# Merging two 256-column steps of a layer into one of 512 columns

## The chip, the cores and the metric

The kernel runs on one core of a Trainium2 chip. The metric is the device time of one execution in microseconds; each version is run several times and the median is compared. Besides, one execution of each version is recorded by the hardware profiler, and the rows shown below come from that.

## The reference

Three stages follow each other, all in fp32. Attention has 4 batches of 8 heads with 576 positions of width 64; of each row of scores only the 32 largest are kept before the softmax. Its output is laid out as 2304 tokens of width 512. Two feed-forward layers follow: layer 1 has 512 to 2048 to 512 with a piecewise function between, layer 2 is gated, with 512 to 1536 to 512.

```
scores = scale * q @ k^T;  kth = 32nd largest of each row
attn = softmax(where(scores >= kth, scores, -1e9));  a = attn @ v
x = a.transpose(0, 2, 1, 3).reshape(2304, 512)
h = x @ w_in
g = where(h >= 1, h, where(h <= -1, 0, (h + 1)**2 / 4));  x2 = g @ w_out
out = (silu(x2 @ w_gate) * (x2 @ w_val)) @ w_out2
```

## The kernel before, in words

**Numbers.** Each fp32 operand of a layer's matmul is split into a high and a low half of TensorE's fp32r type (tile `w`, 128 x 2 x 512), and a product takes three matmuls: high by high, low by high, high by low (`PASSES`). `hilo` (L797 on ACT for the high half, L799 on POOL for the low one) makes the split of activations, `convert` (L762 to L774) that of weights. A converted weight tile is kept in DRAM (`ws_...`) and loaded again, 512 KB, by every later step that needs it (`weight`).

**Attention.** It runs in 32 units: batch, block of query tiles, pair of heads. The blocks of batches 0 to 2 are query tiles (0, 1) and then (2, 3, 4), 256 and 320 columns; those of batch 3 the other way round. A unit has four or five score tiles, 144 in all. For each, PE makes 128 x 576 scores in a pair of PSUM banks `pS` (L612; there are two such pairs), DVE finds the 32nd largest with four MAX8 (L626) and three MATCH_REPLACE8 (L636) and masks with it (L640), ACT takes the exponential (L633). PE then transposes (L687 to L707), multiplies by the values (L567, L569), and the result goes to DRAM as `xs` (store `xs<-y`), by units.

**Layers.** The 2304 tokens are cut into sub-blocks of columns, seven of 256 and a last one, number 7, of 512 (`SUBS`). The list `STEPS` gives the layer steps in program order: layer 1 and 2 of 0, of 1, of 2, then layer 1 of 3, layer 1 of 4, layer 2 of (3, 4), layer 1 of 5, layer 1 of 6, layer 2 of (5, 6), layer 1 of 7, layer 2 of 7. A step's input of layer 1 is loaded from `xs` (`t<-xs`) and needs all four units (pairs of heads) of the attention blocks that its columns touch.

A PSUM bank `pM` holds 512 columns. Where a step has 256 columns, `lanes` puts two units of the wide dimension side by side in one bank (F = 2); where it has two sub-blocks of 256, the two stand side by side (F = 1). In either case `proj` (matmuls at L877) goes through the lanes one by one, four slices k of 128 and three passes each, so that every matmul of such a step has 256 columns. Only sub-block 7 has matmuls of 512 columns there. Behind `proj` of layer 1 come relu, square and gmax (L936, L938, L940) and the split; four finished groups of 128 make a slab, for which `x2_part` multiplies by the second matrix (L913) in the same lanes. Its sums go through `accumulate` (L807 to L815) into `big`, of which there are two; after the last slab `hilo` splits the sum into one wide buffer for each bank of 512 columns, and `self.x2` notes where each slice of each sub-block lies. For a single sub-block of 256 columns a buffer thus holds two slices of it side by side.

Layer 2 projects with gate and value weights (also L877), combines (L996, L998, L1008), splits, and `out_part` (L974) multiplies 128 rows at a time by 512 columns. The rings that matter: 15 wide buffers `w` for weights, inputs and split activations, two banks `pM`, two `big`.

**Order.** Nothing of the order is written by hand. `Plan` collects all operations with modelled durations; `forward` is a list schedule by priority with rings that are handed out in order of creation; `backward` schedules the reversed graph, and its begins are the priorities of the next forward round. `schedule` makes one forward plan from fixed priorities and up to four rounds from backward ones, and keeps the shortest by the model. Each engine then executes its instructions in that fixed order, and all transfers are issued in order on SP's queue.

Of the kernel before, what the change touches and what calls it, by code (L numbers as in the profile page):

```python
# [54 lines left out]
class Op:  # L55
    __slots__ = ("eng", "dur", "fn", "deps", "prio", "seq", "opens", "bufs", "left", "users", "ready", "start", "end", "lat", "tag")


class Plan:
# [9 lines left out]
    def __init__(self):  # L69
        self.ops = []  # L70
        self.rings = []

    def ring(self, *a, **k):
        r = Ring(*a, **k)
        self.rings.append(r)
        return r

    def op(self, eng, dur, fn, reads=(), writes=(), prio=5, tag="", lat=None):
        o = Op()
        o.eng, o.dur, o.fn, o.prio, o.seq, o.tag = eng, dur, fn, self.PRI.get(tag, prio), len(self.ops), tag  # L80
        o.lat = self.LAT if lat is None else lat
        deps = set()
# [119 lines left out]
    def backward(self):  # L202
# [37 lines left out]
        while True:  # L240
# [30 lines left out]
            while events and events[0][0] <= now + 1e-9:  # L271
# [10 lines left out]
                for d in ops[s].deps:  # L282
                    heapq.heappush(events, (now + (0.0 if ops[d].eng == ops[s].eng == "PE" else ops[d].lat), 1, d))

    def schedule(self):

        best, least = self.forward(), self.length
        for _ in range(self.ROUNDS):
            begin = self.backward()
            if begin is None:  # L290
                break
            for o in self.ops:
                o.prio = -begin[o.seq]
# [11 lines left out]
class Kernel:  # L305
    SUBS = (256, 256, 256, 256, 256, 256, 256, 512)
    STEPS = ((1, (0,)), (2, (0,)), (1, (1,)), (2, (1,)), (1, (2,)), (2, (2,)), (1, (3,)), (1, (4,)), (2, (3, 4)),
             (1, (5,)), (1, (6,)), (2, (5, 6)), (1, (7,)), (2, (7,)))

    BLOCKS = (((0, 1), (2, 3, 4)), ((0, 1), (2, 3, 4)), ((0, 1), (2, 3, 4)), ((2, 3, 4), (0, 1)))  # L310
    KV = 4
    AV_POOL = True

    SAME, SWAP = (slice(0, 128), slice(0, 128), 0), ((slice(0, 64), slice(64, 128), 1), (slice(64, 128), slice(0, 64), 1))
# [19 lines left out]

    SB, FN, PS = 0.043, 0.136, 0.065

# [18 lines left out]
    def build(self):  # L355
# [29 lines left out]
        self.p_m = R("pM", [128, 512], F32, 4 - self.PT_BANKS, "P")  # L385
        self.xdeps = {}
        self.attention()
# [3 lines left out]
    def attention(self):  # L391
# [4 lines left out]
        def ready(u):  # L396
            b, hp, blk = units[u]
            if blk == 0:
                state["kv", b, hp] = self.prep(b, hp)
            state["q", u] = self.prep_q(b, hp, self.BLOCKS[b][blk])  # L400

        ready(0)
# [37 lines left out]

    def prep(self, b, hp):

        nc, p, T = self.nc, self.p, self.t
        kT = self.r_kT.new()
        V = self.r_v.new()

        raw = self.load_raw(T["k"], b, hp)
# [21 lines left out]
        raw = self.load_raw(T["v"], b, hp)  # L469
        self.split(raw, V)  # L470
        return kT, V

# [81 lines left out]
    def outputs(self, b, hp, blk, V, PT, rs, rc):  # L554
# [29 lines left out]
        p.op("POOL", self.pool(N), lambda: nc.gpsimd.tensor_tensor(  # L584
            out=y[:, 0:N], in0=y[:, 0:N], in1=rb[:, 0:N], op=OP.mult), [rb], [(y, None)], 2, "norm")
        key = (hp, b, blk)
        xs = self.t["xs"][key]
# [139 lines left out]

    def convert(self, ring, kind, f, early=False):

# [28 lines left out]
        def flat():  # L758
            return W[:].rearrange("p s n -> p (s n)").bitcast(F32) if ring is not None else W[:]


        p.op("ACT", self.act(512, self.SB), lambda: nc.scalar.activation(  # L762
            out=word(0), in_=cv[:].bitcast(U16).rearrange("p (n t) -> p n t", t=4)[:, :, 1], func=AF.Copy,
            scale=2.0 ** -13, bias=2.0 ** -14 - 0.5), [], [(cv, 0)], 3, tag + "cvl")
        p.op("ACT", self.act(512, self.SB), lambda: nc.scalar.activation(
            out=ct[:], in_=word(1, F32), func=AF.Sign), [(cv, 1)], [ct], 3, tag + "cvs")
        p.op("DVE", self.dve(512), lambda: nc.vector.scalar_tensor_tensor(  # L767
            out=word(0), in0=word(1), scalar=3, in1=word(0),
            op0=OP.logical_shift_left, op1=OP.bitwise_or), [(cv, 1)], [(cv, 0)], 3, tag + "cvt")
        p.op("POOL", self.pool(512), lambda: nc.gpsimd.tensor_tensor(  # L770
# [23 lines left out]

    def hilo(self, src, dst, n, prio=3, off=0, key=None):
        nc, p = self.nc, self.p
        p.op("ACT", self.act(n, self.SB), lambda: nc.scalar.activation(out=dst[:, 0, 0:n], in_=src[:, off:off + n], func=AF.Copy),  # L797
             [(src, key)], [(dst, 0)], prio, "hi")
        p.op("POOL", self.pool(n), lambda: nc.gpsimd.tensor_tensor(  # L799
            out=dst[:, 1, 0:n], in0=src[:, off:off + n], in1=dst[:, 0, 0:n].bitcast(F32), op=OP.subtract),  # L800
            [(src, key), (dst, 0)], [(dst, 1)], prio, "lo")

# [31 lines left out]
    def moe(self):  # L834
# [5 lines left out]
        for f in range(self.HELD[0]):  # L840
            self.held["moe_w_in", f] = self.convert(self.r_w, "moe_w_in", f)
            if f < self.HELD[1]:
                self.held["moe_w_out", f] = self.convert(self.r_w, "moe_w_out", f)
# [3 lines left out]
        for u in units[:e1] + units[n1:n1 + e2]:  # L847
            self.convert(None, *u, early=True)
        self.later = units[n1 + e2:][:self.PRE]
# [24 lines left out]

# [7 lines left out]
    def layer1(self, subs):  # L882
        nc, p, T = self.nc, self.p, self.t
        F, lanes, w = self.lanes(subs)
        X = {}
        for kk in range(KC // F):
            xf = self.r_t.new()
            x = self.r_w.new()
# [12 lines left out]
        def x2_part(slab):  # L901
            for f in range(4 * slab, 4 * slab + 4):
                WO[f] = self.weight(self.r_w, "moe_w_out", f)
            for jj in range(KC // F):
                ps = self.p_m.new()
                for u, i, at, n in lanes:
                    for q in range(4):
                        f = 4 * slab + q
                        bank, gat = self.place(subs, f)[i]

                        def mms(f=f, q=q, j=jj * F + u, at=at, n=n, ps=ps, g=G[bank], gat=gat):
# [3 lines left out]
                        p.op("PE", self.mm(n, 3), mms, [WO[f], G[bank]] + [(ps, 0)] * (at > 0), [(ps, at)], 5, "x2")  # L915
                if jj % 2 == 0 and slab == 0:
# [196 lines left out]
```

## Time and profile before

| what | value |
|---|---|
| median of three runs | 1344.08 us (1342.28 to 1344.23) |
| the profiled execution's own time | 1339.11 us |
| its span, first to last instruction | 1337.3 us |
| PE, DVE, ACT, POOL busy | 91%, 77%, 65%, 59% |
| mean granted TensorE clock | 0.962 |
| DMA | 329 MB, 246 GB/s on the mean |

Times are microseconds. PE is TensorE's matmul, PEld its weight load, DVE is VectorE, ACT is ScalarE, POOL is GpSimd, SP is the engine whose queue issues the transfers. L877 is line 877 of the kernel before. The duration of one matmul in a row reaches from its start to its modelled end and overlaps the next one; a matmul's pitch is read where many follow back to back.

### The profile page before, as it was taken

To read this page: it belongs to the slowest core of one execution; us is meant where nothing else is said; L and a number is where in the kernel's file an instruction comes from. 1 tells how busy PE (TensorE), PEld (TensorE's weight loads), DVE (VectorE), ACT (ScalarE), POOL (GpSimd) and SP (SyncE) were. 2 spreads that over 40 slices of the span, in tenths; PEclk is the share of its full clock that TensorE was granted. 3 is DMA by queue.
4 is the path that set the end of the run, shared out by engine and by line. 5 is a ranking of instruction groups with operands and counts; after the bars stand their busy time and mean duration, and the time that the engine had idled before them with its cause. 6 is when DMAs were issued, how large, how long until landed. Compare 5 with 4: busy or idle time off the path is not lost.

```text
span 1337.3 us, 24475 instructions
## 1 busy us (share of the span) xinstructions
PE 1220.9 (91%) x8408; PEld 1126.8 (84%) x8408; DVE 1032.1 (77%) x2066; ACT 875.2 (65%) x1916; POOL 785.7 (59%) x821
## 2 busy tenths in 40 slices
PE   2566588998899999999999999999999999999998
PEld 1445388887799999998999999999999999877887
DVE  5989999999999999999999988999999212122222
ACT  6888799888877678776778777668775321342211
POOL 8977669799956466765577755646554313223111
PEclk9965689999999999999999999999999999999999
DMA  8878778989868796878686844367668554655454
GB/s 294 271 263 282 238 269 279 350 291 326 290 229 308 243 346 216 341 258 304 224 306 244 309 138 167 94 207 278 231 260 312 196 195 184 210 206 198 146 189 157
DMA packets 138188, 329.29 MB, mean 246 GB/s; under 512 B 21200, under 2 KB 67792, under 8 KB 138064
## 3 DMA queue, kind: packets, MB, share of 16 engines
q1 hardware_dynamic: 138064, 327.73, 69.3%
q8 instruction: 66, 1.08, 0.3%
q14 instruction: 58, 0.48, 0.1%
HBM read 282.59 MB, written 45.09 MB: 245 GB/s over the span
## 4 chain that ended last, share of the span: by engine, by line
PE 67%; DVE 9%; ACT 8%; DMA 8%; POOL 4%; issue 3%; SPq 0%; DVEq 0%; ACTq 0%; POOLq 0%
PE pM L877 31%; PE pM L913 12%; PE pM L974 10%; PE pS L612 4%; PE pT L567 4%; DVE v L626 3%; DVE R L636 3%; PE pT L687 3%; DVE cv L767 2%; DMA w<-ws_moe_w_in 1%; DMA cv<-in_moe_w_in_dram 1%; DMA w<-ws_moe_w_out 1%; ACT qT L489 1%; POOL ct L770 1%; ACT cv L762 1%
## 5 line engine op out<-in xcount | busy, mean ns | idle before, releaser
L877 PE MATMUL pM<-w,w 128*128 128x256 f32 (+1 forms) x3840 | 564.4, 300 | 3.2 <-POOL w L799 1.8
L877 PEld LDWEIGHTS pM<-w,w 128*128 128x128 f32 x3840 | 512.1, 192 | 25.2 <-POOL w L799 2.7
L799 POOL TENSOR_TENSOR w<-t,w 128x512 fp32r<-128x512 f32 x144 | 186.9, 1301 | 267.4 <-ACT w L797 240.5
L626 DVE MAX8 v<-R 128x8 f32<-128x576 f32 x432 | 314.8, 748 | 1.1
L913 PE MATMUL pM<-w,w 128*128 128x256 f32 (+1 forms) x1536 | 228.6, 300 | 4.0 <-DVE t L940 2.0
L676 POOL TENSOR_TENSOR PT<-F,PT 128x384 fp32r<-128x384 f32 (+2 forms) x192 | 176.3, 927 | 72.5 <-ACT F L674 66.6
L913 PEld LDWEIGHTS pM<-w,w 128*128 128x128 f32 x1536 | 203.4, 190 | 16.1 <-DVE t L940 4.9
L636 DVE MATCH_REPLACE8 R<-v,R 128x576 f32<-128x576 f32 x288 | 213.3, 741 | 0.0
L974 PE MATMUL pM<-w,w 128*128 128x512 f32 x648 | 160.9, 396 | 2.0 <-DVE t L998 0.9
L797 ACT ACTIVATE w<-t 128x512 fp32r<-128x512 f32 x144 | 91.1, 637 | 94.9 <-DVE t L1008 74.6
L974 PEld LDWEIGHTS pM<-w,w 128*128 128x128 f32 x648 | 118.1, 188 | 25.8 <-POOL w L774 1.6
L626 DVE MAX8 v<-pS 128x8 f32<-128x576 f32 x144 | 109.1, 758 | 32.8 <-PE pS L612 30.2
L612 PE MATMUL pS<-kT,qT 128*128 128x288 f32 x512 | 104.7, 328 | 18.4 <-DVE E L640 16.0
L633 ACT ACTIVATE E<-pS,nb 128x576 f32<-128x576 f32 x144 | 107.3, 745 | 21.1 <-DVE R L636 12.2
L687 PE MATMUL pT<-idf,E 128*128 128x128 f32 x512 | 97.5, 298 | 24.7 <-ACT qz L501 7.8
L640 DVE SCALAR_TENSOR_TENSOR E<-pS,v,E 128x576 f32<-128x576 f32 x144 | 115.7, 803 | 0.4
L998 DVE SCALAR_TENSOR_TENSOR t<-t,pM 128x512 f32<-128x512 f32 x54 | 36.8, 681 | 95.9 <-ACT t L996 95.7
L672 ACT ACTIVATE PT<-pT 128x384 fp32r<-128x384 f32 (+2 forms) x192 | 87.8, 460 | 32.5 <-PE pT L687 18.1
L636 DVE MATCH_REPLACE8 R<-v,pS 128x576 f32<-128x576 f32 x144 | 107.5, 746 | 0.0
L770 POOL TENSOR_TENSOR ct<-ct,cv 128x512 int32<-128x512 int32 x68 | 92.0, 1357 | 22.5 <-DVE cv L767 9.9
L612 PEld LDWEIGHTS pS<-kT,qT 128*128 128x128 f32 x512 | 83.2, 210 | 24.8 <-DVE E L640 20.7
L687 PEld LDWEIGHTS pT<-idf,E 128*128 128x128 f32 x512 | 66.2, 151 | 35.0 <-ACT qT L489 9.3
(83 smaller groups left out, 1772.3 us busy)
## 6 DMA issues: line engine op xcount, KB each, us to landing
w<-ws_moe_w_out SPq DMA_DIRECT2D x184, 512.0 KB, 6.1
w<-ws_moe_w_in SPq DMA_DIRECT2D x118, 512.0 KB, 5.5
w<-ws_moe_w_gate SPq DMA_DIRECT2D x67, 512.0 KB, 5.7
w<-ws_moe_w_val SPq DMA_DIRECT2D x66, 512.0 KB, 6.3
cv<-in_moe_w_out_dram SPq DMA_DIRECT2D x28, 512.0 KB, 4.9
cv<-in_moe_w_in_dram SPq DMA_DIRECT2D x16, 512.0 KB, 5.1
ws_moe_w_out<-w SPq DMA_DIRECT2D x16, 512.0 KB, 5.0
ws_moe_w_out<-cv SPq DMA_DIRECT2D x12, 512.0 KB, 3.4
```

Of the source, the lines that this page charges most:

```text
L612: nc.tensor.matmul(ps[:, j, 0:288], l(), kT[:, hh, at + j * 288:at + (j + 1) * 288], start=k == 0, stop=k == len(lhs) - 1)
L626: p.op("DVE", self.dve(576) + (0 if k else self.PS), lambda: nc.vector.max(out=v8[:, h, k, :], in_=rr() if k else sc()), [Rb if k else ps] ...
L633: p.op("ACT", self.act(576, self.FN - self.SB), lambda h=h, sc=sc, ee=ee: nc.scalar.activation(out=ee(), in_=sc(), func=AF.Exp, bias=nb[:, ...
L636: p.op("DVE", self.dve(576) + 0.06 + (0 if k else self.PS), lambda h=h, k=k, sc=sc, rr=rr: nc.vector.match_replace(out=rr(), in_to_replace ...
L640: p.op("DVE", self.dve(576) + 0.06 + self.PS, lambda h=h, sc=sc, ee=ee: nc.vector.scalar_tensor_tensor(out=ee(), in0=sc(), scalar=v8[:, h, ...
L676: p.op("POOL", self.pool(n), lambda: nc.gpsimd.tensor_tensor(out=dst(1), in0=src(F), in1=dst(0).bitcast(F32), op=OP.subtract), [F, (PT, (0 ...
L687: fn = (lambda ps=ps, m=m, h=h, c=c: nc.tensor.transpose(ps[:, m * 128:(m + 1) * 128], Sb[:, h, 64 * h + c * 128:64 * h + (c + 1) * 128], ...
L770: p.op("POOL", self.pool(512), lambda: nc.gpsimd.tensor_tensor(out=ci(), in0=ci(), in1=word(0), op=OP.add), [(cv, 0)], [ct], 3, tag + "cvadd")
L799: p.op("POOL", self.pool(n), lambda: nc.gpsimd.tensor_tensor(out=dst[:, 1, 0:n], in0=src[:, off:off + n], in1=dst[:, 0, 0:n].bitcast(F32), ...
L877: nc.tensor.matmul(ps[:, at:at + n], W[:, w, k * 128:(k + 1) * 128], x[:, s, xat:xat + n], start=k == 0 and j == 0, stop=k == KC - 1 and j ...
L913: nc.tensor.matmul(ps[:, at:at + n], WO[f][:, v, j * 128:(j + 1) * 128], g[:, s, gat:gat + n], start=q == 0 and m == 0, stop=q == 3 and m ...
L974: nc.tensor.matmul(ps[:], a[:, s, at:at + 128], WO[f][:, v, :], start=q == 0 and m == 0, stop=q == 3 and m == 2)
```

## The change

Sub-blocks 5 and 6 are one step of layer 1. Where two neighbouring lanes belong to the same unit and their inputs adjoin in the same buffer, the new function `joined` makes them one lane, and `proj` and `x2_part` then issue one matmul of 512 columns for two of 256. So that the input of layer 2 of (3, 4) adjoins too, layer 1 of 3 splits each slice of its result into the left half of a buffer of its own, and layer 1 of 4 fills the right half. `hilo` has a column offset for the destination.

```diff
-             (1, (5,)), (1, (6,)), (2, (5, 6)), (1, (7,)), (2, (7,)))
+             (1, (5, 6)), (2, (5, 6)), (1, (7,)), (2, (7,)))
+    JOIN = True
...
-    def hilo(self, src, dst, n, prio=3, off=0, key=None):
+    def hilo(self, src, dst, n, prio=3, off=0, key=None, to=0):
         nc, p = self.nc, self.p
-        p.op("ACT", self.act(n, self.SB), lambda: nc.scalar.activation(out=dst[:, 0, 0:n], in_=src[:, off:off + n], func=AF.Copy),
-             [(src, key)], [(dst, 0)], prio, "hi")
+        p.op("ACT", self.act(n, self.SB), lambda: nc.scalar.activation(out=dst[:, 0, to:to + n], in_=src[:, off:off + n], func=AF.Copy),
+             [(src, key)], [(dst, (0, to))], prio, "hi")
...
+    @staticmethod
+    def joined(lanes, where):
+
+        out = []
+        for u, i, at, n in lanes:
+            x, xat = where(u, i)
+            if out and out[-1][0] == u and out[-1][3] is x and out[-1][1] + out[-1][2] == at and out[-1][4] + out[-1][2] == xat:
+                out[-1][2] += n
+            else:
+                out.append([u, at, n, x, xat])
+        return out
...
-        for u, i, at, n in lanes:
+        both = [self.joined(lanes, lambda u, i, k=k: X[k, i]) for k in range(KC)]
+        for m in range(len(both[0])):
             for k in range(KC):
-                x, xat = X[k, i]
+                u, at, n, x, xat = both[k][m]
...
                 if slab == FF1 // 512 - 1:
-                    x = self.r_w.new()
-                    self.hilo(acc[jj // 2], x, w, off=off, key=jj % 2)
+                    pair = [s for layer, s in self.STEPS if layer == 2 and subs[0] in s][0]
+                    if pair == subs or not self.JOIN:
+                        x = self.r_w.new()
+                        self.hilo(acc[jj // 2], x, w, off=off, key=jj % 2)
+                        for u, i, at, n in lanes:
+                            self.x2[jj * F + u, i] = (x, at)
+                        continue
+
                     for u, i, at, n in lanes:
-                        self.x2[jj * F + u, i] = (x, at)
+                        j, to = jj * F + u, sum(self.SUBS[s] for s in pair if s < i)
+                        if to == 0:
+                            self.x2[j, i] = (self.r_w.new(), 0)
+                        x = self.x2[j, pair[0]][0]
+                        self.x2[j, i] = (x, to)
+                        self.hilo(acc[jj // 2], x, n, off=off + at, key=jj % 2, to=to)
```

The loop over lanes of `x2_part` is changed as that of `proj`. `schedule` keeps the first plan made from backward priorities even if the plan from fixed priorities was shorter, and from there on the shortest:

```diff
         best, least = self.forward(), self.length
+        first = None
         for _ in range(self.ROUNDS):
...
-            if self.length < least:
-                best, least = order, self.length
+            if self.length < least or first is None:
+                best, least, first = order, self.length, [o.prio for o in self.ops]
```

The rest of the diff adds switches that are off (`rush`, `FIRST`, `QFIRST`, `DIRECT`, `VIA`, `BANKED`, `AHEAD`, `PORT` = 0) and splits `prep` into its key and value parts, called one after the other as before.

## Rows read from the trace of the kernel before

**Rows 1.** The page's first lines: span, and busy time of each engine.

```profile
span 1337.3 us, 24475 instructions
...
PE 1220.9 (91%) x8408; PEld 1126.8 (84%) x8408; DVE 1032.1 (77%) x2066; ACT 875.2 (65%) x1916; POOL 785.7 (59%) x821
```

**Rows 2.** Windows: stretch, length, busy (count) of PE, PEld, DVE, ACT, POOL; clock, DMA.

```profile
60.00:180.00 120.00, 72.19 (x304) 57.72 (x303) 110.73 (x216) 98.45 (x207) 89.47 (x87) 0.62 0.76 255
...
200.00:400.00 200.00, 181.78 (x1343) 168.25 (x1342) 194.69 (x381) 173.59 (x381) 171.66 (x167) 0.98 0.84 293
400.00:932.00 532.00, 527.34 (x4094) 509.72 (x4093) 498.99 (x1052) 392.96 (x922) 337.51 (x387) 1.00 0.70 250
...
1046.00:1143.00 97.00, 97.00 (x683) 91.32 (x682) 20.07 (x30) 20.14 (x35) 20.94 (x18) 1.00 0.51 176
```

**Rows 3.** The chain of waits behind attention: start, us, what.

```profile
1045.95 23.04 PE pM L877 x192
1068.99 10.91 PE pM L974 x48
```

**Rows 4.** Timeline of SP's queue: stores and loads of attention's output, start and us.

```profile
806.30 0.32 SPq L351 DMA_DIRECT2D xs<-y  x1
...
895.09 2.32 SPq L351 DMA_DIRECT2D t<-xs  x5
...
920.02 0.37 SPq L351 DMA_DIRECT2D xs<-y  x1
...
928.50 3.00 SPq L351 DMA_DIRECT2D t<-xs  x5
...
945.77 0.32 SPq L351 DMA_DIRECT2D xs<-y  x1
...
952.00 0.32 SPq L351 DMA_DIRECT2D t<-xs  x1
```

**Rows 5.** Timeline of POOL: the last low half of sub-block 6's input.

```profile
954.51 1.30 POOL L799 TENSOR_TENSOR w<-t,w 128x512 fp32r<-128x512 f32 x1 [0.53 <-ACT w L797]
```

**Rows 6.** Groups by shape, PE from 952 us: count, busy, mean ns, idle before.

```profile
L877 PE MATMUL pM<-w,w 128*128 128x512 f32 x480 | 110.9, 390 | 0.7 <-DVE t L998 0.7
L877 PE MATMUL pM<-w,w 128*128 128x256 f32 x792 | 99.6, 284 | 0.0
L974 PE MATMUL pM<-w,w 128*128 128x512 f32 x288 | 66.6, 390 | 0.1
L913 PE MATMUL pM<-w,w 128*128 128x512 f32 x192 | 45.9, 394 | 1.2 <-DVE t L940 1.0
L913 PE MATMUL pM<-w,w 128*128 128x256 f32 x330 | 43.4, 286 | 0.5 <-DMA w<-ws_moe_w_out 0.5
```

**Rows 7.** Timeline of DVE: the last mask of batch 3's first block.

```profile
928.69 0.80 DVE L640 SCALAR_TENSOR_TENSOR E<-pS,v,E 128x576 f32<-128x576 f32 x1
```

**Rows 8.** Groups by shape, DVE up to 930 us.

```profile
L640 DVE SCALAR_TENSOR_TENSOR E<-pS,v,E 128x576 f32<-128x576 f32 x128 | 102.8, 803 | 0.3
...
L940 DVE SCALAR_TENSOR_TENSOR t<-pM,t 128x512 f32<-128x512 f32 x43 | 29.2, 680 | 2.9 <-ACT t L938 2.2 <-PE pS L612 0.6
L998 DVE SCALAR_TENSOR_TENSOR t<-t,pM 128x512 f32<-128x512 f32 x30 | 20.3, 676 | 2.5 <-ACT t L996 2.3
L1008 DVE SCALAR_TENSOR_TENSOR t<-t,pM 128x512 f32<-128x512 f32 x30 | 20.3, 676 | 2.1 <-PE pM L877 2.0
```

**Rows 9.** Waits of DVE, 400 to 930 us: total us, times, longest.

```profile
DVE v L626 <- PE pS L612: 23.7, 36, 2.6
```

**Rows 10.** Timeline of PE: the last matmuls of layer 2 of (3,4).

```profile
915.65 0.86 PE L974 MATMUL pM<-w,w 128*128 128x512 f32 x3
```

**Rows 11.** Waits of PE, 400 to 952 us: the longest in total.

```profile
PE pM L877 <- POOL w L799: 1.8, 3, 0.8
```

**Rows 12.** The page's DMA issues: count, KB each, median us to landing.

```profile
w<-ws_moe_w_out SPq DMA_DIRECT2D x184, 512.0 KB, 6.1
```

**Rows 13.** Groups by shape, whole span: a POOL subtraction of 256 columns.

```profile
L437 POOL TENSOR_TENSOR hq<-raw,hq 128x256 fp32r<-128x256 f32 x16 | 12.3, 768 | 3.6 <-ACT hq L435 3.5
```

More of the change, by code (lines that the diff above doesn't have):

```diff
@@ L55 @@
 class Op:
-    __slots__ = ("eng", "dur", "fn", "deps", "prio", "seq", "opens", "bufs", "left", "users", "ready", "start", "end", "lat", "tag")
+    __slots__ = ("eng", "dur", "fn", "deps", "prio", "seq", "opens", "bufs", "left", "users", "ready", "start", "end", "lat", "tag", "rush")
 class Plan:
@@ L81, in op @@
         o.lat = self.LAT if lat is None else lat
+        o.rush = 1e6 * self.rush
+        o.prio -= o.rush
         deps = set()
@@ L297, in schedule @@
                 break
-            if self.length < least:
-                best, least = order, self.length
+            if self.length < least or first is None:
+                best, least, first = order, self.length, [o.prio for o in self.ops]
+        if self.AHEAD:
+            for o, prio in zip(self.ops, first):
+                o.prio = prio - self.AHEAD.get(o.tag, 0)
+            best, least = self.forward(), self.length
         self.length = least
@@ L312 @@
     AV_POOL = True
+    DIRECT = False
+    JOIN = True
+    QFIRST = False
+    VIA, BANKED = 0, 0
+    FIRST = False
     SAME, SWAP = (slice(0, 128), slice(0, 128), 0), ((slice(0, 64), slice(64, 128), 1), (slice(64, 128), slice(0, 64), 1))
@@ L397, in ready @@
             b, hp, blk = units[u]
+            self.p.rush = self.FIRST and u == 0
             if blk == 0:
-                state["kv", b, hp] = self.prep(b, hp)
+                kT = self.prep_k(b, hp)
+                if not self.QFIRST:
+                    state["kv", b, hp] = kT, self.prep_v(b, hp)
             state["q", u] = self.prep_q(b, hp, self.BLOCKS[b][blk])
+            self.p.rush = False
+            if blk == 0 and self.QFIRST:
+                state["kv", b, hp] = kT, self.prep_v(b, hp)
         ready(0)
@@ L439, in split, with prep_k @@
             [raw, (hl, 0)], [(hl, D)], 2, "spl_lo")
-    def prep(self, b, hp):
+    def prep_k(self, b, hp):
         nc, p, T = self.nc, self.p, self.t
         kT = self.r_kT.new()
-        V = self.r_v.new()
         raw = self.load_raw(T["k"], b, hp)
@@ L467, in prep, with prep_v @@
                 out=kT[:, 1, at:at + 64], in_=ps[:, 192:256], func=AF.Copy), [ps], [(kT, "b%d" % i)], 2, "kTe")
-        raw = self.load_raw(T["v"], b, hp)
-        self.split(raw, V)
-        return kT, V
+        return kT
+    def prep_v(self, b, hp):
+        V = self.r_v.new()
+        self.split(self.load_raw(self.t["v"], b, hp), V)
+        return V
     def prep_q(self, b, hp, qts):
@@ L585, in outputs @@
             out=y[:, 0:N], in0=y[:, 0:N], in1=rb[:, 0:N], op=OP.mult), [rb], [(y, None)], 2, "norm")
+        if (b, blk) == (0, 0) and self.DIRECT:
+            kk, u = divmod(hp, 512 // N)
+            if u == 0:
+                self.x0[kk] = self.r_w.new()
+            x, at = self.x0[kk], u * N
+            p.op("ACT", self.act(N, self.SB), lambda: nc.scalar.activation(
+                out=x[:, 0, at:at + N], in_=y[:, 0:N], func=AF.Copy), [y], [(x, (0, u))], 2, "hi")
+            p.op("POOL", self.pool(N), lambda: nc.gpsimd.tensor_tensor(
+                out=x[:, 1, at:at + N], in0=y[:, 0:N], in1=x[:, 0, at:at + N].bitcast(F32), op=OP.subtract),
+                [y, (x, (0, u))], [(x, (1, u))], 2, "lo")
+            return
         key = (hp, b, blk)
@@ L759, in flat, with bits @@
             return W[:].rearrange("p s n -> p (s n)").bitcast(F32) if ring is not None else W[:]
+        low = self.p_m.new() if bank else cv
+        def bits():
+            return low[:].bitcast(I32) if bank else word(0)
         p.op("ACT", self.act(512, self.SB), lambda: nc.scalar.activation(
-            out=word(0), in_=cv[:].bitcast(U16).rearrange("p (n t) -> p n t", t=4)[:, :, 1], func=AF.Copy,
-            scale=2.0 ** -13, bias=2.0 ** -14 - 0.5), [], [(cv, 0)], 3, tag + "cvl")
+            out=bits(), in_=cv[:].bitcast(U16).rearrange("p (n t) -> p n t", t=4)[:, :, 1], func=AF.Copy,
+            scale=2.0 ** -13, bias=2.0 ** -14 - 0.5), [(cv, 0)] if bank else [], [(low, 0)], 3, tag + "cvl")
         p.op("ACT", self.act(512, self.SB), lambda: nc.scalar.activation(
             out=ct[:], in_=word(1, F32), func=AF.Sign), [(cv, 1)], [ct], 3, tag + "cvs")
-        p.op("DVE", self.dve(512), lambda: nc.vector.scalar_tensor_tensor(
-            out=word(0), in0=word(1), scalar=3, in1=word(0),
-            op0=OP.logical_shift_left, op1=OP.bitwise_or), [(cv, 1)], [(cv, 0)], 3, tag + "cvt")
+        p.op("DVE", self.dve(512) + (self.PS if bank else self.PORT), lambda: nc.vector.scalar_tensor_tensor(
+            out=word(0), in0=word(1), scalar=3, in1=bits(),
+            op0=OP.logical_shift_left, op1=OP.bitwise_or), [(cv, 1)] + [(low, 0)] * bank, [(cv, 0)], 3, tag + "cvt")
         p.op("POOL", self.pool(512), lambda: nc.gpsimd.tensor_tensor(
@@ L840, in moe @@
         for f in range(self.HELD[0]):
-            self.held["moe_w_in", f] = self.convert(self.r_w, "moe_w_in", f)
+            self.held["moe_w_in", f] = self.convert(self.r_w, "moe_w_in", f, bank=self.BANKED > 0)
             if f < self.HELD[1]:
-                self.held["moe_w_out", f] = self.convert(self.r_w, "moe_w_out", f)
+                self.held["moe_w_out", f] = self.convert(self.r_w, "moe_w_out", f, bank=self.BANKED > 0)
         units = [u for u in self.units() if u not in self.held]
@@ L846, in moe @@
         e1, e2 = self.EARLY
-        for u in units[:e1] + units[n1:n1 + e2]:
-            self.convert(None, *u, early=True)
+        for i, u in enumerate(units[:e1] + units[n1:n1 + e2]):
+            self.convert(self.r_w if i < self.VIA else None, *u, early=True, bank=i < self.BANKED - sum(self.HELD))
         self.later = units[n1 + e2:][:self.PRE]
@@ L886, in layer1 @@
         for kk in range(KC // F):
+            if subs == (0,) and self.DIRECT:
+                for u, i, at, n in lanes:
+                    X[kk * F + u, i] = (self.x0[kk], at)
+                continue
             xf = self.r_t.new()
@@ L905, in x2_part, with mms @@
                 ps = self.p_m.new()
-                for u, i, at, n in lanes:
+                both = [self.joined(lanes, lambda u, i, f=f: (G[self.place(subs, f)[i][0]], self.place(subs, f)[i][1]))
+                        for f in range(4 * slab, 4 * slab + 4)]
+                for z in range(len(both[0])):
                     for q in range(4):
                         f = 4 * slab + q
-                        bank, gat = self.place(subs, f)[i]
-                        def mms(f=f, q=q, j=jj * F + u, at=at, n=n, ps=ps, g=G[bank], gat=gat):
+                        u, at, n, g, gat = both[q][z]
+                        def mms(f=f, q=q, j=jj * F + u, at=at, n=n, ps=ps, g=g, gat=gat):
                             for m, (v, s) in enumerate(self.PASSES):
```

18 lines of the change are left out of this document (11 added, 7 removed).

## The prediction

> **What bounds the kernel now.** Read the page's first lines first [rows 1]: the profiled execution spans 1337.3 us (1339.11 us in the metric, so 1.8 us lie around the span), PE is busy for 91% of it and DVE for 77%. An average hides two regimes, so the windows come next [rows 2]. From 400 to 932 us PE is busy for 527 of 532 us and DVE for 499: attention's top-k work on DVE and the two layers' matmuls on PE go side by side and both are nearly full. From 1046 on attention is over: PE is busy for 97 of 97 us, DVE for 20, and only PE matters.
>
> So the end is PE's sum of work plus the time in which PE had nothing to do, and a PE saving counts only while PE has work that is ready. The question for this change is therefore double: how much PE work goes, and whether PE must now wait for attention, since the merged step needs sub-block 6 where half of it needed only sub-block 5.
>
> **Part 1, wider matmuls.** The chain of waits gives true pitches, as it follows PE back to back [rows 3]: 192 matmuls of 256 columns took 23.04 us, 0.1200 us each; 48 of 512 columns took 10.91 us, 0.2273 us each. Two of 256 merged into one of 512 save 0.2400 - 0.2273 = 0.0127 us. (The "mean ns" of the grouped rows, 284 and 390, overlap and are no pitches.) Merged are: layer 1 of (5,6), projections 16 x 4 x 3 = 192 and x2 part 192, so 384 pairs; layer 2 of (3,4) and of (5,6), 24 x 4 x 3 = 288 pairs each. Together 960 pairs, 12.2 us of PE: 4.9 + 3.7 + 3.7.
>
> The Trainium skill, "TensorE: Matmul & The Clock Gate", section "Back-to-back issue gap", gives N / 2.4 ns plus 2.5 ns for a matmul at the full clock. That would be 109.2 and 215.8 ns, and a merged pair would save 2.5 ns, 2.4 us in all. The trace does not agree: 120.0 and 227.3 ns stand in it at a granted clock of 1.00, so the row's 12.7 ns per pair is used.
>
> **Part 2, what the merged step waits for.** Sub-block 5 (columns 1280 to 1535) ends inside batch 2, sub-block 6 (1536 to 1791) reaches 64 columns into the first block of batch 3. On the queue of SP [rows 4] the last store of batch 2 goes out at 806.30, yet sub-block 5 is loaded only at 895.09: it was never short of data. Sub-block 6's loads go out from 928.50; the last but one store of batch 3's first block is at 920.02, the last at 945.77, and the last load at 952.00. Its low half on POOL ends at 954.51 + 1.30 = 955.8 [rows 5]; nine of the first twelve matmuls (9 x 0.2273 = 2.0 us) don't need it, so the step can start at T = 954. Before, layer 1 of 5 filled PE from about 915 on; now that work too waits for T.
>
> Left for PE after T, all at 512 columns: layer 1 of (5,6) 384, layer 2 of (5,6) 288 + 144, layer 1 of 7 384, layer 2 of 7 288 + 144, in sum 1632 x 0.2273 = 371.0 us. What else lies there I take from the kernel before at 952 us [rows 6]: 792 + 330 matmuls of 256 (134.6 us) and 480 + 288 + 192 of 512 (218.2 us) make 352.9 us; to the end are 385.3 us; the rest, 32.4 us, is attention's last four units and stalls. At 954 call it 32. With T where it is, the span is 954 + 371 + 32 = 1357, 20 us longer. The point from which it is a gain: T = 1337.3 - 403 = 934, 20 us earlier.
>
> **Part 3, how far T can move.** The last mask of batch 3's first block ends at 929.5 [rows 7], 24.5 us ahead of T; before it DVE must do its 128 of 144 score tiles, the conversions, and the vector work of the steps up to layer 2 of (3,4): 40 gmax and 60 of layer 2. Up to 930 the rows count 43 gmax and 30 on each of the two layer-2 lines [rows 8], so just 3 x 0.68 = 2.0 us of DVE's work belonged to sub-block 5 and goes behind. Everything else stays, unless matmuls of (3,4) are put off behind T, which costs PE there what it gives. What is left is DVE's idle time. It is 33.0 us from 400 to 932, 6.2%, of which 23.7 us is waiting for the score matmuls [rows 2, 9]. Bounds: 0 to 33 us. From 200 to 400 DVE idles just 2.7% [rows 2]; reaching that after 400 would win 532 x 0.035 = 19 us. But the score matmuls wait because PE's queue is full, and until the earlier steps are done it stays so: the last matmuls of layer 2 of (3, 4) run at 915.65 [rows 10]. I take 12 us, between nothing and that row. T = 954 - 2 - 12 = 940, and the span 940 + 371 + 32 = 1343, 5.7 us longer. Both ends: T = 921 gives 1324 (about PE's own floor, 1337.3 - 12.2 = 1325), T = 954 gives 1357.
>
> Seen from PE: its pool of earlier steps ends about 4 us sooner, near 912 (the 3.7 us of (3,4), lost again), then only attention's matmuls feed it until T, and the 8.6 us saved in the two steps of (5,6) pay for part of that.
>
> **Edits costed at nothing.** The merged step loads its 32 weight tiles once, not twice: 32 loads of 512 KB fewer. The longest of PE's waits from 400 to 952 is for POOL, 1.8 us in all [rows 11]; fewer loads give nothing, at most the 0.5 us that x2 matmuls waited for one after 952 [rows 6]. The number of relu, square, gmax, split and accumulate instructions for 5 and 6 is the same, 16 of 512 columns each. For 3 and 4 each split in halves of 256: POOL pays 4 x 0.77 (a subtraction of 256 columns [rows 13]) for 2 x 1.30 us [rows 5] per sub-block, 0.5 us more; ACT, by the same pattern, about as much. Both engines are off the path (ACT and POOL 65% and 59% [rows 1]); uncovered it would be under 2 us. Of the 15 wide buffers four, not two, are held from the end of layer 1 of 3. The loads for layer 1 of 4 then have two slots less of lead; a load takes 6.1 us to land [rows 12], so 0 to 6 us of PE stalls, inside the stretch in which PE will have time to spare: 0, and 6 in a case where it has none. The 16 loads of the merged step's input stand in SP's queue where those of 6 did, the same wait behind the same store. The planner's new rule takes the first backward plan even if the forward one is shorter. Which one was taken before no row shows; every engine's order may shift a little, and I give that 3 us either way.
>
> **Rivals.**
> 1. *Attention catches up* (the other side). With more depending on batch 3's first block, the planner ranks its scores above matmuls of the pool, whose order has 20 to 30 us to give. For it: the 23.7 us of waits for scores, ACT and POOL with room, the 24.5 us tail with gaps (a wait of PE's queue and POOL's in each hop). Against: DVE at 94%, its work before T fixed. It decides from T = 934; at T = 926 the span is 1329, a median of 1336, and at the floor 1332.
> 2. *The clock falls in the lull.* Where PE had attention alone, from 60 to 180 us, it was busy for 60% and the granted clock was 0.62 [rows 2], a mix of 2.4 and 1.2 GHz. If the lull ahead of T is like that, the transposes and output matmuls in the tail (about 5 us of PE) take twice as long, and the merged step starts at half clock, some 3 us: 8 us on top of the forecast, span 1351, median 1358. Against: full clock everywhere since 200 us, with attention spread between other matmuls. The Trainium skill, same page, section "Why this matters for your kernels", says to leave no idle gaps of PE between bursts, since the clock then drops back; the row from 60 to 180 agrees as far as it goes.
> 3. *T moves just enough* (931 to 937): saving and wait cancel, median 1341 to 1347.
> That the merge doesn't happen I rule out: both lanes of (5,6) have one unit, one buffer and adjoining columns, which is all that `joined` asks.
>
> **How the numbers follow.** The median of three runs, 1344.08, is 5.0 us over the profiled execution; the difference of 5.7 us is put on the median: 1349.8, say 1350. Chances: forecast (T 937 to 954) 0.45; rival 1 0.31; rival 2 0.08; rival 3 0.16. About 0.2%, 2.7 us, is what a measurement can tell from no change. Faster 0.31, within 0.16, slower 0.53. The likeliest case's own range is 1347 to 1364; for 8 in 10 I reach into rival 1 nearly to PE's floor: 1333 to 1363.
>
> **What would show it.** Counts: 960 matmuls fewer, L877 and L913 with 512 columns 1248 and 384 times, 32 weight loads fewer. The step itself: if the forecast holds, the last store of batch 3's first block lies near 932, the first wide projections follow it by 8 us, and ahead of them PE shows idle pieces or attention alone for 20 to 30 us, most of it behind 900 us; after them 403 us to the end. If that store goes out by 923 and no lull is seen, rival 1 holds and I was wrong on DVE's reserve. A granted clock under 0.9 in a slice near 920 is rival 2. If pitches in (3,4) or (5,6) aren't 0.227, part 1 is wrong.

## The result, and the profile after

The change makes the kernel slower: 1363.91 us median (1358.81 to 1366.28) against 1344.15, a ratio of 1.0143 with a 95% interval of 1.0116 to 1.0169, about 20 us. Forecast were 1350 and the right direction; the time lies just past the end of the range, 1363. The profiled execution took 1366.28 us, 2 us above the median, and that of the kernel before was 5 us below its own; so the two spans below lie 27 us apart where the medians lie 20.

The page after: span, busy times, and the clock in 40 slices.

```profile
span 1364.5 us, 22522 instructions
...
PE 1223.2 (90%) x7448; PEld 1082.6 (79%) x7448; DVE 1029.7 (75%) x2066; ACT 877.6 (64%) x1920; POOL 786.0 (58%) x825
...
PEclk9966589999899999999999999999899999999999
```

PE has 960 matmuls fewer than before [rows 1], yet its busy time is the same, and 141 us of the span are idle for PE, 25 more than before. Busy time doesn't tell that less is to be done, as a narrow matmul's recorded duration overlaps its neighbour's. The Trainium skill, "Trainium Kernel Development and Optimization", section "Performance Expectations", warns of just this: matmul busy time says little of how near a kernel is to its limit, because matmuls are pipelined. Here PE's rows agree: 1220.9 us with 8408 matmuls, 1223.2 with 7448.

The merge itself is there as forecast. Groups by shape, PE over the whole span: proj is L934 now, x2_part L976, out_part L1048.

```profile
L934 PE MATMUL pM<-w,w 128*128 128x512 f32 x1248 | 302.9, 395 | 1.1 <-DVE t L1072 0.7 <-ACT t L855 0.2
...
L976 PE MATMUL pM<-w,w 128*128 128x512 f32 x384 | 94.3, 397 | 1.2 <-DVE t L1014 1.0
```

1248 and 384 wide matmuls, as counted ahead. Their pitch in the chain of waits (start, us, what) is the one of [rows 3]:

```profile
1077.44 21.82 PE pM L934 x96
```

21.82 us for 96 wide matmuls, 0.2273 each, where 192 narrow ones took 23.04 us. So the 12.2 us of PE are real work gone, and everything else has to explain 32 us. (The formula of the Trainium skill, "TensorE: Matmul & The Clock Gate", section "Back-to-back issue gap", which that section gives for a single matmul by itself, comes to 0.2158; the measurement decides.)

The first place to look is where the merged step starts. SP's queue after, beside [rows 4] (start, us):

```profile
816.63 0.32 SPq L371 DMA_DIRECT2D xs<-y  x1
...
923.63 0.32 SPq L371 DMA_DIRECT2D xs<-y  x1
...
953.76 0.33 SPq L371 DMA_DIRECT2D xs<-y  x1
955.54 0.32 SPq L371 DMA_DIRECT2D t<-xs  x1
```

Batch 2's last store is at 816.63, 10 us later than before; the last store that sub-block 6 needs is at 953.76, 8 us later than before, where the forecast wanted it some 14 us earlier. Windows, columns as in [rows 2], first of the kernel before, then of the one after:

```profile
700.00:800.00 100.00, 99.04 (x812) 97.72 (x810) 94.20 (x199) 77.95 (x187) 69.04 (x78) 1.00 0.66 238
...
895.00:930.00 35.00, 35.00 (x247) 32.78 (x246) 32.30 (x71) 26.57 (x59) 22.57 (x26) 1.00 0.75 261
930.00:965.00 35.00, 34.83 (x289) 34.61 (x288) 34.07 (x73) 27.20 (x63) 20.86 (x25) 1.00 0.72 256
```

```profile
700.00:800.00 100.00, 93.86 (x717) 89.38 (x716) 91.14 (x194) 77.89 (x189) 70.35 (x83) 0.98 0.68 244
...
920.00:930.00 10.00, 8.38 (x41) 6.94 (x40) 9.23 (x20) 8.22 (x17) 7.54 (x10) 0.83 0.22 62
930.00:965.00 35.00, 26.72 (x131) 20.70 (x131) 31.60 (x69) 22.80 (x52) 21.39 (x26) 0.93 0.57 176
...
955.00:960.00 5.00, 3.55 (x13) 2.61 (x13) 4.96 (x12) 4.06 (x8) 3.17 (x4) 0.69 0.65 203
...
965.00:970.00 5.00, 5.00 (x22) 4.30 (x22) 5.00 (x10) 3.13 (x7) 3.76 (x5) 0.79 0.01 3
```

Two losses stand here. From 700 to 800 us, mostly layer 1 of 4, PE is busy for 93.9 us where it was busy for 99.0 before. And from 930 to 965 it is busy for 26.7 of 35 us, where it was full before: the lull ahead of the merged step. Its end, on PE's timeline, and on POOL's the low half of the last input that the step needs:

```profile
957.00 1.33 PE L651 MATMUL pS<-kT,qT 128*128 128x288 f32 x4 [1.44 <-DVE E L679]
...
958.83 2.59 PE L934 MATMUL pM<-w,w 128*128 128x512 f32 x6
964.15 1.33 PE L651 MATMUL pS<-kT,qT 128*128 128x288 f32 x4 [2.73 <-DVE E L679]
...
966.19 4.13 PE L934 MATMUL pM<-w,w 128*128 128x512 f32 x15
```

```profile
958.85 1.27 POOL L843 TENSOR_TENSOR w<-t,w 128x512 fp32r<-128x512 f32 x1
```

The last wide input is split by 960.1. Less the 2 us that the forecast took off, this is T = 958, where 954 was read before and 940 forecast; 18 wide matmuls that don't need that input ran in pieces from 938.8 on, 6 more at 958.83. Then the score matmuls (L651), queued ahead on PE, wait another 2.73 us for DVE's mask, and the layer's matmuls stand behind them; the wide run begins at 966.2. Four score matmuls take 1.33 us at 957 and 964, and 0.77 at 952.92: in the lull the granted clock had fallen, to 0.69 from 955 to 960 and 0.79 from 965 to 970, a mix of 2.4 and 1.2 GHz; before the fall PE had been busy for 2.95 of the 5 us from 950 to 955. The page's slice from 955 to 989 shows it too, as the last 8 in its line.

### The profile page after: what moved, and what is told of

Read it like the earlier page. It is cut to its first block, busy times and chain, and to the rows that moved or that the text cites. A ratio compares the mean times of both kernels' runs of the same rounds, so it can differ in the third digit from the quotient of the medians.

```text
span 1364.5 us, 22522 instructions
## 1 busy us (share of the span) xinstructions
PE 1223.2 (90%) x7448; PEld 1082.6 (79%) x7448; DVE 1029.7 (75%) x2066; ACT 877.6 (64%) x1920; POOL 786.0 (58%) x825
## 4 chain that ended last, share of the span: by engine, by line
PE 68%; DVE 8%; ACT 8%; DMA 6%; POOL 6%; issue 3%; SPq 0%; DVEq 0%; POOLq 0%; ACTq 0%
PE pM L934 33%; PE pM L976 11%; PE pM L1048 9%; PE pS L651 5%; PE pT L594 4%; DVE v L665 3%; PE pT L726 3%; DVE R L675 2%; POOL ct L814 2%; DMA cv<-in_moe_w_in_dram 1%; DVE cv L811 1%; ACT qT L516 1%; ACT E L672 1%; PE pT L596 1%; POOL w L818 1%
## 5 line engine op out<-in xcount | busy, mean ns | idle before, releaser
L934 PE MATMUL pM<-w,w 128*128 128x256 f32 (+1 forms) x3072 | 560.0, 334 | 6.4 <-DMA w<-ws_moe_w_in 3.0
L934 PEld LDWEIGHTS pM<-w,w 128*128 128x128 f32 x3072 | 466.8, 193 | 56.7 <-POOL w L843 3.0
L976 PE MATMUL pM<-w,w 128*128 128x256 f32 (+1 forms) x1344 | 229.8, 320 | 4.7 <-DMA w<-ws_moe_w_out 2.6
L976 PEld LDWEIGHTS pM<-w,w 128*128 128x128 f32 x1344 | 192.3, 190 | 23.7 <-DVE t L1014 3.5
L1048 PE MATMUL pM<-w,w 128*128 128x512 f32 x648 | 163.6, 401 | 3.3 <-POOL w L818 1.6
L1048 PEld LDWEIGHTS pM<-w,w 128*128 128x128 f32 x648 | 119.8, 191 | 28.7 <-POOL w L818 2.4
L651 PE MATMUL pS<-kT,qT 128*128 128x288 f32 x512 | 105.2, 331 | 28.2 <-DVE E L679 25.7
L726 PE MATMUL pT<-idf,E 128*128 128x128 f32 x512 | 98.3, 301 | 30.6 <-ACT qT L516 12.2
L651 PEld LDWEIGHTS pS<-kT,qT 128*128 128x128 f32 x512 | 85.2, 212 | 37.1 <-DVE E L679 31.7
```

Source lines behind the costliest of these rows:

```text
L651: nc.tensor.matmul(ps[:, j, 0:288], l(), kT[:, hh, at + j * 288:at + (j + 1) * 288], start=k == 0, stop=k == len(lhs) - 1)
L726: fn = (lambda ps=ps, m=m, h=h, c=c: nc.tensor.transpose(ps[:, m * 128:(m + 1) * 128], Sb[:, h, 64 * h + c * 128:64 * h + (c + 1) * 128], ...
L934: nc.tensor.matmul(ps[:, at:at + n], W[:, w, k * 128:(k + 1) * 128], x[:, s, xat:xat + n], start=k == 0 and j == 0, stop=k == KC - 1 and j ...
L1048: nc.tensor.matmul(ps[:], a[:, s, at:at + 128], WO[f][:, v, :], start=q == 0 and m == 0, stop=q == 3 and m == 2)
```

## The experiments

Two theories. *Gate*: the merged step waits for sub-block 6, and attention can't be hurried enough. *Buffers*: with `JOIN`, the four half-filled wide buffers that layer 1 of 3 opens take slots from layer 1 of 4 (and those of 5 from 6), whose weights then come late. With both parts switched off, the changed source gives the instruction order of the kernel before on every engine; the new rule in `schedule`, the finer keys in `hilo` and the unused switches do nothing by themselves, and the two parts are all there is to test. What the planner itself expects can be had without a run, as the modelled length of its plan: 1328.6 us for the kernel before and 1344.6 for the changed one. Its model thus has 16 of the 20 us. The plan from fixed priorities is longer than the first backward one in both (1353.2 and 1332.3, 1373.7 and 1346.2), so the new rule decides nothing.

**The shared buffers alone** (e1_join_only).

```diff
-             (1, (5, 6)), (2, (5, 6)), (1, (7,)), (2, (7,)))
+             (1, (5,)), (1, (6,)), (2, (5, 6)), (1, (7,)), (2, (7,)))
```

> The pairs of layer 2 keep their common buffers and matmuls of 512 columns, but layer 1 of 5 and of 6 are two steps again. Theory G (the gate: the merged step waits for sub-block 6's input): without the merge nothing waits longer than before, so 576 pairs at 0.0127 us come off PE, about 7 us faster than before, near 1337. Theory W (the buffers: four half-filled wide buffers held from the end of layer 1 of 3 leave layer 1 of 4 too few slots for its weights): slower than before although PE has 7 us less to do, by 3 to 12 us, and PE's waits for weight loads or its low rate show between 700 and 800 us.

1355.85 us, ratio 1.0091 (1.0076 to 1.0106): slower by 12 us with 7.3 us less to do. Had the gate been the only cost, this would have been faster than before. The buffers cost, which the prediction had priced at nothing. Here both pairs hold them, (3, 4) and (5, 6); in the changed kernel just (3, 4) does.

**The merge alone** (e2_merge_only).

```diff
-    JOIN = True
+    JOIN = False
```

> Layer 1 of (5, 6) is one step, but 3 and 4 do not share buffers, and layer 2 of (3, 4) has matmuls of 256 columns as before. G: 15 to 22 us slower than before (1359 to 1366), the last load of the merged step's input still near 954, and a lull of PE ahead of it. W: most of the loss goes with the shared buffers; within 5 us of before.

1354.70 us, ratio 1.0091 (1.0069 to 1.0112): 11 us slower, between the two expectations, but clear of noise: the merge costs by itself as well. The last store that the step needs is at 939.13 here, 6.6 us ahead of before; the last load at 940.91.

**The gate undone** (e3_early_input).

```diff
                 for b, blk, off, a, m in self.pieces(self.cols[i], n):
                     a += at
+                    if subs == (5, 6) and b == 3:
+                        b, blk = 2, 1
```

> The changed kernel, but the 64 columns of sub-block 6 that come from batch 3 are read from batch 2's last block (that part of the output is then another one's), so the merged step needs no score of batch 3. G: the wait is gone, layer 1 of (5, 6) starts as soon as PE is done with the steps before, and the 12 us of wider matmuls come through: 1332 to 1340, at least 20 us faster than the changed kernel. W: the buffers still cost; 1350 or more.

1348.54 us, ratio 1.0036 (1.0025 to 1.0048): 15.4 us faster than the changed kernel, where at least 20 were expected, and not faster than before. The gate is worth 15 us, and it isn't all.

**Attention ahead of everything** (e4_ahead), to see how early batch 3's first block can be.

```diff
-    AHEAD = {}
+    AHEAD = dict.fromkeys("kTt qTt ... qk max8 nb exp mrep mask ... xst ldqkv".split(), 100.0)
```

> The changed kernel with every operation of attention ranked 100 us ahead in the planner. If DVE has a reserve of some 20 us ahead of the merged step (what the forecast counted on half of), the last store of batch 3's first block moves from 954 to 935 or earlier. If DVE's own work sets it, the store moves by under 12 us although attention now has the first claim on every engine, and the earlier layer steps are pushed behind it, so that the whole is slower than the changed kernel by 20 us or more.

1417.13 us in a single run; neither expectation holds cleanly, as the store moves far but the whole is 53 us slower than the changed kernel. SP's queue:

```profile
935.09 0.32 SPq L371 DMA_DIRECT2D xs<-y  x1
...
992.58 5.98 SPq L371 DMA_DIRECT2D t<-xs  x5
```

The store is at 935.09: 19 us ahead of the changed kernel, but only 10.7 ahead of before, although the planner now ranks attention first. The merged step's input is loaded from 992.6 to 1023, as PE is far behind with the earlier steps by then. The forecast's point of gain lay 20 us ahead of before, and this order doesn't reach it. It is no upper bound, though: the buffers are still held here, and DVE is busy for just 488.7 us from 400 to 930, less than the 497.0 of before.

**Wide matmuls without held buffers** (e5_late_join). A pair's sums stay in `big` until the second sub-block is done; then both are split into fresh wide buffers. Layer 1 of 5 and of 6 are separate.

```diff
-        self.x2 = {}
+        self.x2, self.sums = {}, {}
...
-                        if to == 0:
-                            self.x2[j, i] = (self.r_w.new(), 0)
-                        x = self.x2[j, pair[0]][0]
-                        self.x2[j, i] = (x, to)
-                        self.hilo(acc[jj // 2], x, n, off=off + at, key=jj % 2, to=to)
+                        self.sums[j, i] = (acc[jj // 2], n, off + at, jj % 2, to)
+                        if i == pair[-1]:
+                            x = self.r_w.new()
+                            for s in pair:
+                                big, m, o, key, to = self.sums.pop((j, s))
+                                self.hilo(big, x, m, off=o, key=key, to=to)
+                                self.x2[j, s] = (x, to)
```

> Layer 1 of 5 and 6 separate, pairs of layer 2 with matmuls of 512 columns as in e1_join_only, but a pair's sums stay in big (which has two buffers) until the second sub-block is done, and both are split then; no half-filled wide buffer is held. If e1's loss comes from the held buffers, it goes, and the 576 narrower pairs' saving of 7 us comes through: 1334 to 1340, with PE's layer work between 700 and 800 us back near 68 us. If it comes from the width of the matmuls, from the split in halves or from the planner's order alone, this stays slower than before, 1350 or more.

1340.87 us, ratio 0.9963 (0.9951 to 0.9976). This beats both kernels: 15.0 us faster than e1_join_only with the same matmuls, and 4 to 5 of the 7 us come through. PE's groups by shape from 700 to 800 us show where, first in the kernel before, in e1_join_only and in this one (count | busy, mean ns | idle before):

```profile
L877 PE MATMUL pM<-w,w 128*128 128x256 f32 x379 | 52.0, 287 | 0.0
L913 PE MATMUL pM<-w,w 128*128 128x256 f32 x195 | 26.5, 287 | 0.7 <-DVE t L940 0.7
```

```profile
L976 PE MATMUL pM<-w,w 128*128 128x256 f32 x234 | 33.7, 289 | 0.3 <-ACT big L851 0.2
L934 PE MATMUL pM<-w,w 128*128 128x256 f32 x192 | 26.4, 290 | 2.9 <-DMA w<-ws_moe_w_in 2.9
L934 PE MATMUL pM<-w,w 128*128 128x512 f32 x39 | 11.1, 413 | 0.0
```

```profile
L976 PE MATMUL pM<-w,w 128*128 128x256 f32 x221 | 29.9, 287 | 0.1
L934 PE MATMUL pM<-w,w 128*128 128x256 f32 x192 | 25.8, 285 | 0.0
L934 PE MATMUL pM<-w,w 128*128 128x512 f32 x87 | 22.5, 400 | 0.0
```

By pitch that is 574 x 0.1200 = 68.9 us of layer work before, 426 x 0.1200 + 39 x 0.2273 = 60.0 with the held buffers, and 413 x 0.1200 + 87 x 0.2273 = 69.3 with the late split. Attention's matmuls in that stretch are, but for one or two, the same in number. What held the layers up is seen on SP's queue, where a weight's load waits until PE is done with the buffer that it will fill. Waits of SP from 700 to 800 us (total us, times, longest), in the same order:

```profile
SPq L351 <- PE pM L913: 20.6, 7, 7.5
...
SPq L351 <- PE pM L877: 4.6, 4, 2.0
```

```profile
SPq L371 <- PE pM L976: 26.1, 8, 9.2
SPq L371 <- PE pM L934: 13.5, 8, 3.2
```

```profile
SPq L371 <- PE pM L976: 13.1, 8, 5.5
...
SPq L371 <- PE pM L934: 7.6, 6, 2.5
```

25.2, 39.6 and 20.7 us. On PE 6.3 us of the stretch are idle in e1_join_only, against 1.0 before, and just one row puts some of it down to a weight:

```profile
PE pM L934 <- DMA w<-ws_moe_w_in: 2.9, 2, 2.0
```

**Held buffers without wide matmuls** (e6_narrow_join).

```diff
-            if out and out[-1][0] == u and out[-1][3] is x and ...
+            if False and out[-1][0] == u and out[-1][3] is x and ...
```

> The shared buffers of e1_join_only without its wide matmuls (joined lanes are not merged), and layer 1 of 5 and 6 separate. If holding four half-filled buffers is the cost, it stays and the saving is gone: 5 to 8 us above e1_join_only, 1360 to 1364. If the wide matmuls were the cost, it falls to before's 1344.

1360.29 us, ratio 1.0115 (1.0097 to 1.0133), 4.4 us above e1_join_only: the cost stays, the saving goes, somewhat less of it than expected.

**The buffers held idle in the kernel before** (e9_hold_two).

```diff
-        self.x2 = {}
+        self.x2, self.idle = {}, []
...
                     x = self.r_w.new()
                     self.hilo(acc[jj // 2], x, w, off=off, key=jj % 2)
+                    if subs in ((3,), (5,)):
+                        d = self.r_w.new()
+                        p.op("ACT", 0.1, lambda d=d: nc.scalar.activation(
+                            out=d[:, 0, 0:1], in_=self.one[:], func=AF.Copy), [], [d], 3, "hi")
+                        self.idle.append(d)
+                    if subs in ((4,), (6,)):
+                        d = self.idle.pop(0)
+                        p.op("ACT", 0.1, lambda d=d, x=x: nc.scalar.activation(
+                            out=d[:, 0, 1:2], in_=d[:, 0, 0:1].bitcast(F32), func=AF.Copy), [(x, 0)], [d], 3, "hi")
```

> The kernel before, all its matmuls and buffers as they were, but from the end of layer 1 of 3 to the end of layer 1 of 4, and likewise from 5 to 6, two more of the 15 wide buffers are held idle (an ACT write of one column opens each, another one releases it). If holding the two extra buffers is the whole cost of the shared halves, this loses what e6_narrow_join loses, 12 to 18 us over before (1356 to 1362), with PE's layer work between 700 and 800 us near 60 us and SP waiting longer for PE to free buffers. If the cost is in the split by halves or the placing, it stays within 3 us of before.

1360.07 us, ratio 1.0118 (1.0099 to 1.0137). Two of 15 buffers, held without any use in two stretches, cost 16 us. The layer work from 700 to 800 is 515 x 0.1200 = 61.8 us, and SP waits 34.5 us for PE:

```profile
L877 PE MATMUL pM<-w,w 128*128 128x256 f32 x293 | 40.1, 287 | 2.2 <-DVE t L1007 1.3 <-DMA w<-ws_moe_w_in 0.9
L913 PE MATMUL pM<-w,w 128*128 128x256 f32 x222 | 31.4, 289 | 1.6 <-ACT big L807 0.8 <-DMA w<-ws_moe_w_out 0.7
```

```profile
SPq L351 <- PE pM L913: 25.8, 12, 9.0
...
SPq L351 <- PE pM L877: 8.7, 7, 2.5
```

The second stretch, from 5 to 6, shows as the first does. PE from 1000 to 1100 us, in the kernel before and here:

```profile
1000.00:1100.00 100.00, 99.46 (x788) 97.13 (x787) 46.98 (x92) 37.16 (x75) 32.84 (x33) 1.00 0.61 228
```

```profile
1000.00:1100.00 100.00, 94.24 (x735) 90.82 (x734) 46.77 (x92) 43.37 (x89) 34.62 (x35) 1.00 0.59 216
```

**The changed kernel with the late split** (e7_late_merge): the edit of e5_late_join, layer 1 of (5, 6) merged.

> The changed kernel with 3's and 4's sums split late as in e5_late_join: the merge of layer 1 stays, the held buffers go. Gate: the merged step still waits for batch 3's first block, so about e2_merge_only less the 3.7 us of (3, 4), if those count at all ahead of the gate: 1349 to 1356, 8 to 14 us faster than the changed kernel, slower than before.

1354.79 us, ratio 1.0067 (1.0052 to 1.0083), 9.1 us faster than the changed kernel. The median is that of e2_merge_only: the 3.7 us of (3, 4) lie ahead of the gate and show no gain (the ratios, 1.0067 and 1.0091, leave up to some 3 us open). SP's queue, DVE's wait for scores from 400 to 930, the low half of the last input, and PE's window:

```profile
938.82 0.32 SPq L371 DMA_DIRECT2D xs<-y  x1
...
944.02 0.32 SPq L371 DMA_DIRECT2D t<-xs  x1
```

```profile
DVE v L665 <- PE pS L651: 17.5, 32, 1.1
```

```profile
946.49 1.27 POOL L843 TENSOR_TENSOR w<-t,w 128x512 fp32r<-128x512 f32 x1 [2.29 <-ACT w L841]
```

```profile
930.00:965.00 35.00, 28.43 (x136) 22.95 (x136) 27.54 (x56) 21.99 (x45) 19.18 (x22) 0.85 0.50 162
```

The store is at 938.82, 7 us ahead of before; DVE waits 17.5 us for scores where it was 23.7 [rows 9]. The last input is split by 947.8, so T is 946. And still PE is busy for just 28.4 us of the 35 from 930, at a granted clock of 0.85. This is the gate without the buffers; the fall of the clock is part of its price, and no run separates the two.

**Both undone** (e8_late_early_input): e7_late_merge with the early input of e3_early_input.

> The changed kernel with both suspects taken away: sums split late, and sub-block 6's 64 columns of batch 3 read from batch 2's last block (that part of the output is another one's). If gate and buffers are the whole loss, PE's 12 us come through: 1330 to 1336, 28 to 34 us faster than the changed kernel. If a third cost is in the merged step itself, 1340 or more.

1339.60 us, ratio 0.9965 (0.9952 to 0.9978): 24.3 us faster than the changed kernel, and about 5 us faster than before where 12 were expected. A third cost is left, of some 7 us. A part is seen where the step begins, in the window, on SP's queue with the wait ahead of it, and on PE:

```profile
895.00:930.00 35.00, 32.43 (x181) 26.98 (x180) 31.12 (x68) 28.56 (x70) 27.85 (x32) 1.00 0.62 191
```

```profile
897.27 0.38 SPq L371 DMA_DIRECT2D raw<-in_q_dram  x1
897.71 2.36 SPq L371 DMA_DIRECT2D t<-xs  x5
...
913.40 1.98 SPq L371 DMA_DIRECT2D t<-xs  x3
```

```profile
SPq L371 <- POOL hq L463: 8.3, 1, 8.3
```

```profile
920.46 0.55 PE L726 MATMUL pT<-idf,E 128*128 128x128 f32 x3 [1.20 <-ACT y L602]
...
925.50 0.55 PE L726 MATMUL pT<-idf,E 128*128 128x128 f32 x3 [1.37 <-ACT F L713]
```

The data were stored at 811. The loads go out from 897.7 to 915.4, behind attention's load of queries, for which SP waited 8.3 us until POOL had split earlier ones. PE is then busy for 32.4 of 35 us, where before it was full, and the 2.6 us are two waits of attention's transposes for ACT, behind which the layer's matmuls stand. The rest stays open. Some lies far ahead of any changed step: by 400 us PE had been busy for 291.5 us, 295.1 before, with 929 narrow matmuls of the layers done instead of 947 (2.2 us by pitch). And the merge of layer 1, worth 4.9 us by its matmuls, shows no clear gain over e5_late_join even with its input ready, 1339.60 us against 1340.87; the planner's model has them just as near, 1319.8 and 1320.8 us, so that part was lost in the planned order.

The four kernels with the merge make a table of both causes (median us, ratio to before):

| | buffers held | late split |
|---|---|---|
| waits for sub-block 6 | 1363.91 (1.0143) | 1354.79 (1.0067) |
| input from batch 2 | 1348.54 (1.0036) | 1339.60 (0.9965) |

The gate costs 15.4 us in one column and 15.2 in the other, the held buffers 9.1 and 8.9 us in the rows: they add up. Unmerged, where both pairs hold buffers, they cost 15.0 us (e1_join_only against e5_late_join). The account: -12.2 by pitch, +15.3 gate, +9.0 buffers, +7 left over make +19, and 19.8 were measured. The 7 is what was left in e8_late_early_input, so that the sum closes is no further proof; what the table shows is that the two causes add up.

## Why the prediction was wrong

**The wider matmuls: right in pitch.** 960 pairs, 0.2273 us for a wide one; in layer 2 of (5, 6) the projections behind attention took 63.3 us in 528 narrow matmuls before and 59.9 in 264 wide ones after, 13 ns less for a pair. That all 12.2 us come off the end was not seen: with both causes undone about 5 did.

**What is left behind T: right in size.** From T, measured as in the forecast, to the end are 406 us in the kernel after (958.1 to 1364.5) and 409 in e7_late_merge (945.8 to 1354.5), for 403. The 3 to 6 us more hold the fallen clock and the waits of the queued score matmuls.

**T: the step that failed.** "I take 12 us, between nothing and that row", and T = 940. T was 958. This is 18 of the 21.5 us by which the profiled span, 1364.5, misses the forecast 1343, and two things were wrong in it.

First, the reserve of DVE was put too high, though not absent: 6 of the 18 us. With no buffers held, T came 8 us earlier than before, to 946, and the store 6.6 to 7 (e2_merge_only, e7_late_merge), half of the 14 forecast; with attention ranked ahead of all else the store came 10.7 earlier. The bound of 33 us was idle time. DVE's waits for scores fell by 6.2 us in e7_late_merge, about what the store gained; the 17.5 us that stayed are 32 waits of 0.55 us on the mean. That these are the hop from DVE's mask to PE's next scores and back, and so no reserve, is a reading of the rows and wasn't tried.

Second, "0, and 6 in a case where it has none" for the 15 wide buffers: the other 12 us of T, from 946 in e7_late_merge to 958. This was the mis-sized term: 9 us of the time in the changed kernel. The mechanism (two slots less of lead for the weights) stood in the text, but it was priced by one late load and then covered by PE's spare time in the lull. The lull lies behind 920 and the stall at 700 to 800; PE's time is not spare there. It delayed the earlier layer steps, and attention with them: the changed kernel's store is 15 us later than e7_late_merge's.

**The rivals.** Attention did not catch up by the 20 us that it would have taken. The clock did fall, on top of the gate, and beyond the sign named (under 0.9 near 920): 0.83 from 920 to 930 and 0.69 from 955 to 960 in the kernel after, 0.85 from 930 to 965 in e7_late_merge. So this rival came true beside the likeliest case instead of in its place; its share wasn't measured by itself. The likeliest case was right as a mechanism: "the merged step waits". That T left at 954 would also have given 20 us, the measured loss, is luck: T moved in both directions, 8 us forward by the planner and 12 back by the buffers. So is it that the median misses by only 14 us: the profile before lay 5 us under its median and the one after 2 us over.

**The edits at nothing.** The planner's new rule: nothing, as said. The halves split by 256 weren't tried alone; e5_late_join splits by halves too and still gains, so they can hide in no more than the 2 to 4 us that it lacks. Fewer loads weren't tried alone either, and no gain of theirs shows.

## What to carry to other kernels

A buffer that is opened earlier takes its slots from whatever is prefetched through the same ring: price it by the rate of the stretch it is held in, with the wait of the issuing queue for free buffers as the row to read, not by one late load. Before merging two steps for wider instructions, ask when the later one's input is there, and which engine would have to be faster to make up for it; count idle time on that engine as reserve only where a run shows that it can be used (here some 7 of 33 us could). Where the first of two sums can stay where it is until the second is done, the wide form costs no buffer of that ring. And where a kernel is planned by a model, ask the model first: here it had the loss before any run.

## What the runs showed of the machine that was not expected

Two of 15 wide buffers held idle, from 3 to 4 and again from 5 to 6, cost 16 us (1.2%), while few rows put PE's idle time down to a load: in e9_hold_two 1.6 of the 5.8 us idle from 700 to 800, in e1_join_only 2.9 of 6.3. Attention's matmuls in the stretch are as many as before, so the loss is to be read from the layers' work done there, 60.0 us for 68.9 in e1_join_only, and from the issuing queue's waits, not from one wait of PE.
